# Infini-attention beside a spectral filter: maxima over ScalarE's queue, products with v in two bursts, PSUM banks dealt anew

## The chip, the cores and the metric

One core of a Trainium2 chip runs one program. TensorE (PE, with its weight loads shown as PEld), VectorE (DVE), ScalarE (ACT), GpSimd (POOL) and SyncE (SP, which here only issues DMAs) work side by side, each through its own instructions in order, and wait for each other by semaphores. Matmuls write PSUM, which has 8 banks of 128 x 512 float32; DVE and ACT read it. The metric is the device time of one execution in microseconds, lower is better.

## The reference

Two independent parts whose outputs stand side by side in the last axis. S is 2048, D is 576.

```python
# A: 32 heads of 18, four segments of L = 512
for s in range(4):
    logits = einsum("bhqd,bhkd->bhqk", qs, ks) * scale + causal_mask
    a_dot = einsum("bhqk,bhkd->bhqd", softmax(logits), vs)
    a_mem = einsum("bhld,bhde->bhle", phi(qs), M) / (einsum("bhld,bhd->bhl", phi(qs), z) + 1e-6)
    outs.append(g * a_mem + (1.0 - g) * a_dot)      # g = sigmoid(beta), one per head
    M = M + einsum("bhld,bhle->bhde", phi(ks), vs)
    z = z + phi(ks).sum(over l)
a = concat(outs, heads) @ wo
# B: a filter in frequency
b = irfft2(rfft2(x) * (w_r + 1j * w_i), s=(S, D))
```

## The kernel before

The order of the work is written out by hand: every helper is a generator, and loops step several generators against each other, so the order in the program is the order on each engine. A tile of a pool has a tag with a fixed number of buffers; a new tile of the tag waits until an earlier one has been read by all its readers.

**Stages.** First the forward transform of B (`FFT.forward`, to about 75 us): 16 units u, software-pipelined over 20 steps. `prep` (L118 and on) forms sums and differences eo on DVE, ACT rounds them to eh, and DVE forms the rest el; the third block of eh keeps the rounded value in partitions 0 to 32 and the rest in 64 to 96 (L132, 33 partitions). `f1` multiplies with tables (14 matmuls into two banks), `ev0` (ACT) and `ev1` (DVE) split its result into X0 and X1, `c1` multiplies those (12 matmuls, real and imaginary part in a bank each), and `evz` (ACT, L153) copies them to Z. In step u stand ev0(u-1), evz(u-4), ev1(u-1), f1(u), c1(u-3), with butterfly steps of DVE handed out by a pace counter. PSUM: three pairs for f1 and two single banks for c1.

Then the projections q, k, v of A (to about 283 us), the inverse transform of B together with the start of the attention (to about 357 us), and the attention proper (`attention`, 357 us to the end).

**The attention.** It has 16 units n (segment g = n // 4, eight heads each), halves k = 0 to 31 (four heads each) and steps t = 4k + hh, one head per step. `s1` computes logits with the query on the partitions, ten steps ahead; DVE takes row maxima (L642, L648). `mpath` collects the maxima of four heads (started in the step with hh = 1), PE transposes them (L667, hh = 3), ACT copies them to mts (L670, one buffer), and a DMA (L671) writes them to rows 108 and 109 of the stack Q, so that `s2` subtracts them by matmul, five steps after the transposition at the soonest. `s2` computes logits again with the key on the partitions in three banks (L681; L685 and L686; L690) and ACT takes the exps P0, P1, P2 (L682, L687, L691). After the fourth head POOL zeroes the triangles of P (four selects, L694). `pv` (L709) multiplies by v, four heads side by side in the columns of the array: key block j = 0 two steps after the half's last, j = 1 in the next, j = 3 and 2 in the one after, none in the fourth. `pv_out` copies the sum to U on ACT (L715), `u_dmas` sends it off, `recip` brings back reciprocals of the denominators over DMAs.

A step runs, in this order: two parts of s1 and s2 each (s1 of step t + 10, s2 of step t), pv, `run_bg(1.2)`, the third parts, pv_out, the lanes of reciprocals, `run_bg(0)`. `run_bg` steps the background generators: `den`, `mem1` (memory term), `combine` and `oproj` (output projection) of the segments before. It adds its argument to a counter and does one part when that has reached 1, so every fifth step does a second part, at `run_bg(0)`. PSUM: three banks for s1, three for s2, one for pv and one ("post") for all background parts. s1 has no work left from t = 118 on.

After the steps a drain loop finishes the background, then `last_tile` and `last_proj` finish the last segment, whose reciprocals (rd) come last.

Of the kernel before, what the change touches and what calls it, by code (L numbers as in the profile page):

```python
# [102 lines left out]
class FFT:  # L103
# [4 lines left out]
    def forward(s,xp,cp,pp,wl,xs,consts):  # L108
# [10 lines left out]
        def prep(u,halves=False):  # L119

            x=xin.pop(u)
            eo=xp.tile([128,2,3,128],F32,name="eo",bufs=2)
            h=xp.tile([128,2,3,128],F32R,name="eh",bufs=3)
            for r,op in enumerate((OP.add,OP.subtract)):
                v.tensor_tensor(eo[:,r],x[:,0],x[:,1],op=op)  # L125
                if halves: nc.scalar.copy(h[:,r],eo[:,r])
            if not halves: nc.scalar.copy(h,eo)
            yield
            l=xp.tile([128,2,2,128],F32R,name="el",bufs=3)
            for w in (slice(0,1),slice(1,2)) if halves else (slice(0,2),):  # L130
                v.tensor_tensor(l[:,w],eo[:,w,:2],h[:,w,:2].bitcast(F32),op=OP.subtract)
                v.tensor_tensor(h[64:97,w,2],eo[64:97,w,2],h[64:97,w,2].bitcast(F32),op=OP.subtract)  # L132
            eh[u],el[u]=h,l
            yield
# [16 lines left out]
        def evz(u):  # L151
            a,b=BORD[u]
            for r,p in enumerate(C.pop(u)): nc.scalar.copy(s.Z[:,b,a,r],p[:,:FP])  # L153
        def c1(u):
            a,b=BORD[u]; x=X.pop(u); cc=cw.pop(u)
            for r in range(2):
                p=pp.tile([128,512],F32,name="c1",tag="c1")
                n=0
                for (i,hl) in ((0,0),(0,1),(1,0)):
                    for q in range(2):  # L160
                        k=(0 if q==0 else 2) if r==0 else (1 if q==0 else 0)
                        nc.tensor.matmul(p[:,:FP],cc[:,hl,k*128:(k+1)*128],x[i][:,q],start=n==0,stop=n==5)
                        n+=1
                C.setdefault(u,[]).append(p)
        load(0)
# [219 lines left out]
class ATT:  # L385
# [270 lines left out]
    def mpath(s,k):  # L656

        nc=s.nc; n,qd=divmod(k,2); Q=s.Qs[n%3]
        mx=s.mx.pop(k); mg=s.mg.pop(k)
        nc.vector.tensor_reduce(out=mg[:,:,2:3],in_=mx[:,:,:3],axis=mybir.AxisListType.X,op=OP.max)  # L660
        nc.scalar.copy(mg[:,:,0:1],mx[:,:,3:])
        mh=s.mh; mg=mg.rearrange("p h i -> p (h i)")
        nc.gpsimd.tensor_copy(mh[:,0],mg)
        nc.gpsimd.tensor_tensor(mh[:,1],mg,mh[:,0],op=OP.subtract)
        yield
        pt=s.psm.tile([128,1024],BF,name="mt",tag=s.mtag)[:,:128]
        nc.tensor.transpose(pt,mh.rearrange("p a m -> p (a m)"),s.idb)  # L667
        yield
        mt=s.sm.tile([32,128],BF,name="mts",bufs=1)
        nc.scalar.copy(mt,pt[:32])  # L670
        nc.gpsimd.dma_start(Q[108:110,4*qd:4*qd+4].rearrange("p h (i c) -> p (h i) c",c=128),mt)  # L671
        yield
    def s2(s,t):
# [3 lines left out]
        P=s.P[k]  # L677
# [13 lines left out]
        nc.scalar.activation(P[2][:,hh],p2,AF.Exp,scale=SC)  # L691
        if hh==3:
            def sel(x,pat):
                nc.gpsimd.affine_select(out=x,in_=x,pattern=pat+[[1,128]],compare_op=OP.is_ge,fill=0.0,base=0,channel_multiplier=-1)  # L694
            sel(P[0][:,:,:128],[[0,4]])
            sel(P[1][:,:,:128],[[0,4]])
            sel(P[1][:,:,384:],[[0,4]])
            sel(P[2][:,:,:128],[[0,4]])
        yield
    def pv(s,k,jj):  # L700

        nc=s.nc; n,qd=divmod(k,2); g,G=divmod(n,4)
        P=s.P[k]; vt=s.vs[n]
        if jj==0: s.pvt=s.ps.tile([128,512],F32,name="pv",tag="pv")
        for j in ((0,),(1,),(3,2),())[jj]:
            mv=((P[0],slice(0,512)),(P[1],slice(0,384)),(P[2],slice(0,256)),(P[1],slice(384,512)))[j]
            for hh in range(4):
                h=4*qd+hh
                nc.tensor.matmul(s.pvt[32*hh:32*hh+32,128*j:],vt[:,j,19*h:19*h+32],mv[0][:,hh,mv[1]],start=j==0,stop=j==2,skip_group_check=True)  # L709
# [46 lines left out]
    def den(s,g,lane):  # L756
        nc=s.nc; tp=s.tp
        ds,ds2=[tp.tile([128,512],F32,name=f"ds{i}",tag="ux",bufs=3) for i in range(2)]; ds2=ds2[:32]
        for T,d in ((range(4),ds),((4,),ds2)):
            pd=s.ps.tile([128,512],F32,name="pd",tag="post")  # L760
            for t in T:
                r=126 if t<4 else 72
                nc.tensor.matmul(pd[32*(t%4):32*(t%4)+32],s.zst[g][:r,t],s.pq[g,t][:r],start=True,stop=True,skip_group_check=True)
            nc.scalar.copy(d,pd[:d.shape[0]])
            yield
# [3 lines left out]
        def chain():  # L769
# [3 lines left out]
            yield from s.recip(s.dD[g],s.rdD[g],s.gt,True,"rd",2)  # L773
        lane.append(chain())
    def mem1(s,g,t):
        nc=s.nc; r=126 if t<4 else 72
        pn=s.ps.tile([126,512],F32,name="pn",tag="post")
        nc.tensor.matmul(pn[:r],s.Mst[g][:r,t,:r],s.pq.pop((g,t))[:r],start=True,stop=True)  # L778
# [3 lines left out]
        yield  # L782
        pb=s.ps.tile([126,512],F32,name="pb",tag="post")
        nc.tensor.matmul(pb[:r],s.sel[:,t,:r],s.rc["rd"],start=True,stop=True)
# [15 lines left out]
    def combine(s,g):  # L800
# [14 lines left out]
        for t in range(7+late):  # L815
            if t>1 and not late: high(t-2); low(t-2)
            if t<5:
                r=126 if t<4 else 72; x=xs[t]
                pb=s.ps.tile([126,512],F32,name="pb",tag="post")
                nc.tensor.matmul(pb[:r],s.sel[:,t,:r],s.rc["rr"],start=True,stop=True)  # L820
# [60 lines left out]
    def begin(s,sm,sp,ps1):  # L881
        s.late=[]; s.now=-1
        s.sm,s.sp,s.ps1=sm,sp,ps1
        s.mh=sm.tile([128,8,16],BF,name="mh",bufs=1); s.nc.gpsimd.memset(s.mh,0.0)
        s.mg={};s.mx={};s.m2={};s.P={};s.vs={};s.rc={};s.am={};s.pq={};s.ux={};s.potag="post"
    def prologue(s):
# [20 lines left out]
    def attention(s,tp,ps):  # L907
# [19 lines left out]
        for t in range(133):  # L927
# [24 lines left out]
            steps(a,1)  # L952
            steps(b,1)
            steps(a,1)
            steps(b,1)
# [17 lines left out]
            if qu: qu.pop(0)()  # L973
            run_bg(0)
            s.due(t)
# [142 lines left out]
```

## Time and profile before

| | us |
|---|---|
| median of 3 runs (lowest, highest) | 723.44 (721.72, 724.72) |
| the profiled execution, its own time | 723.62 |
| its span, first to last instruction | 721.9 |
| mean granted clock of TensorE | 0.996 |

Busy shares of the span in 40 slices (tenths; 9 is 90% or more), and the longest pieces by line of the chain that ended last:

```profile
PE   4998999999999999999998999999999999999897
DVE  6999879899699789788587888887566875667433
ACT  3665797585586575444487777777556776567531
POOL 2111000100200112665165334545242762335300
...
PE 75%; DVE 8%; ACT 6%; DMA 5%; issue 3%; POOL 2%; SPq 0%; ACTq 0%; DVEq 0%; POOLq 0%
```

A slice is 18 us. PE is busy nearly everywhere, and the chain is its work for 75% of the span. A busy PE is not PE at its peak: a matmul's record reaches to its modelled end, past the start of the next, so gaps are read from starts in the timeline. A row of the timeline has start and duration in us, engine, line, operation, out<-in, shape, count, and in brackets the idle time before it and what ended that. A row of waits has the waiting instruction, the one waited for, us in total, times, longest.

### The profile page before, as it was taken

To read this page: it belongs to the slowest core of one execution; us is meant where nothing else is said; L and a number is where in the kernel's file an instruction comes from. 1 tells how busy PE (TensorE), PEld (TensorE's weight loads), DVE (VectorE), ACT (ScalarE), POOL (GpSimd) and SP (SyncE) were. 2 spreads that over 40 slices of the span, in tenths; PEclk is the share of its full clock that TensorE was granted. 3 is DMA by queue.
4 is the path that set the end of the run, shared out by engine and by line. 5 is a ranking of instruction groups with operands and counts; after the bars stand their busy time and mean duration, and the time that the engine had idled before them with its cause. 6 is when DMAs were issued, how large, how long until landed. Compare 5 with 4: busy or idle time off the path is not lost.

```text
span 721.9 us, 14482 instructions
## 1 busy us (share of the span) xinstructions
PE 689.0 (95%) x5007; PEld 500.2 (69%) x5007; DVE 551.2 (76%) x1281; ACT 455.2 (63%) x1008; POOL 208.9 (29%) x411
## 2 busy tenths in 40 slices
PE   4998999999999999999998999999999999999897
PEld 4988769879779879999844444444566445664397
DVE  6999879899699789788587888887566875667433
ACT  3665797585586575444487777777556776567531
POOL 2111000100200112665165334545242762335300
PEclk9999999999999999999999999999999999999999
DMA  9884435546363568899547666776546775441142
GB/s 342 268 273 152 132 132 183 176 172 192 102 224 147 176 198 283 204 231 232 166 108 182 172 158 143 177 177 175 128 109 169 177 175 138 111 118 42 34 140 89
DMA packets 83245, 121.06 MB, mean 168 GB/s; under 512 B 11352, under 2 KB 50630, under 8 KB 83036
## 3 DMA queue, kind: packets, MB, share of 16 engines
q1 hardware_dynamic: 76580, 104.11, 50.7%
q0 software_dynamic: 6592, 16.03, 8.1%
q8 instruction: 39, 0.64, 0.4%
q14 instruction: 34, 0.28, 0.1%
HBM read 81.78 MB, written 38.24 MB: 166 GB/s over the span
## 4 chain that ended last, share of the span: by engine, by line
PE 75%; DVE 8%; ACT 6%; DMA 5%; issue 3%; POOL 2%; SPq 0%; ACTq 0%; DVEq 0%; POOLq 0%
PE pj L460 14%; PE pv L709 9%; PE s L638 8%; PE pjv L460 8%; PE po L843 7%; PE i L296 4%; PE i L307 4%; PE s L681 3%; PE s L685 2%; PE pn L778 2%; PE po L872 2%; DVE eo L125 2%; DMA Qs<-mts 2%; PE pm L517 2%; PE s L647 2%
## 5 line engine op out<-in xcount | busy, mean ns | idle before, releaser
L642 DVE CUSTOM_DVE_ANT_0 junk<-s,x 128x512 bf16<-128x512 f32 (+1 forms) x256 | 141.3, 552 | 61.9 <-PE s L638 58.2
L694 POOL TENSOR_SCALAR_AFFINE_SELECT P<-P 128x512 f32<-128x512 f32 x128 | 78.4, 644 | 79.6 <-ACT P L682 72.7
L648 DVE TENSOR_REDUCE mx<-s 128x4 f32<-128x512 f32 x128 | 87.9, 687 | 9.3 <-PE s L647 6.3
L709 PE MATMUL pv<-P,vs 128*32 128x512 f32 (+3 forms) x1024 | 88.8, 442 | 1.0 <-POOL P L694 1.0
L682 ACT ACTIVATE P<-s 128x512 f32<-128x512 f32 x128 | 76.3, 596 | 14.7 <-PE s L681 12.0
L691 ACT ACTIVATE P<-s 128x256 f32<-128x256 f32 x128 | 49.1, 384 | 49.3 <-PE s L690 49.2
L687 ACT ACTIVATE P<-s 128x512 f32<-128x512 f32 x128 | 76.0, 594 | 0.4 <-PE s L686 0.4
L638 PE MATMUL s<-Ks,Qs 108*128 108x384 bf16 (+3 forms) x256 | 69.0, 301 | 1.2 <-DVE mx L648 0.9
L460 PE MATMUL pj<-x,wqkh 128*128 128x512 f32 x162 | 56.5, 409 | 0.0
L638 PEld LDWEIGHTS <-Qs 108*128 108x128 bf16 x320 | 31.5, 99 | 32.8 <-issue 23.4
L206 DVE TENSOR_TENSOR Z<-t,t 128x290 f32<-128x290 f32 (+1 forms) x96 | 48.4, 555 | 0.1
L507 POOL MEMSET vt<- 128x32 f32 x16 | 2.3, 161 | 151.5 <-PE pm L517 124.2
L206 DVE TENSOR_TENSOR t<-Z 128x580 f32<-128x580 f32 x64 | 46.1, 756 | 0.0
L647 PE MATMUL s<-tri,idb 128*128 128x128 bf16 x256 | 43.2, 220 | 0.0
L142 PE MATMUL f<-ftab,eh 128*128 128x290 f32 (+1 forms) x160 | 31.8, 318 | 9.2 <-DMA ftab<-ftab 9.2
L296 PE MATMUL i<-civ,Y 128*128 128x256 f32 (+1 forms) x288 | 39.1, 288 | 0.2 <-POOL Y L281 0.2
L709 PEld LDWEIGHTS pv<-P,vs 128*32 128x32 f32 x1024 | 22.1, 108 | 22.0 <-issue 14.2
L296 PEld LDWEIGHTS i<-civ,Y 128*128 128x128 f32 (+1 forms) x288 | 36.4, 181 | 1.0 <-POOL Y L281 0.4
L638 PE MATMUL s<-Ks,x 108*128 108x384 bf16 (+3 forms) x128 | 35.6, 309 | 0.9 <-DVE mx L648 0.6
L307 PE MATMUL i<-itab,T 128*128 128x290 f32 (+1 forms) x224 | 36.3, 305 | 0.0
L460 PE MATMUL pj<-xh,wqkl 128*128 128x512 f32 x90 | 35.5, 395 | 0.0
L460 PE MATMUL pj<-x,wqkl 128*128 128x512 f32 x90 | 35.5, 395 | 0.0
(202 smaller groups left out, 1813.7 us busy)
## 6 DMA issues: line engine op xcount, KB each, us to landing
qkD<-sp SPq DMA_DIRECT2D x36, 384.0 KB
Ks<-qkD SPq DMA_DIRECT2D x72, 144.0 KB
x<-qkD SPq DMA_DIRECT2D x60, 144.0 KB
Qs<-qkD SPq DMA_DIRECT2D x60, 144.0 KB
xin<-xb SPq DMA_DIRECT2D x16, 384.0 KB
cfw<-cfw POOLq DMA_DIRECT2D x16, 384.0 KB, 4.6
civ<-civ POOLq DMA_DIRECT2D x16, 384.0 KB, 7.4
vs<-vD SPq DMA_DIRECT2D x16, 330.0 KB
```

The source lines that it names most:

```text
L206: v.tensor_tensor(o,a,b,op=op)
L296: nc.tensor.matmul(p[:m,k],Y[i][:,q,c*128:c*128+m],cc[:,hl,o:o+256],start=n==0,stop=n==5)
L307: nc.tensor.matmul(p,x,t,start=n==0,stop=n==6)
L460: s.nc.tensor.matmul(out,a,b,start=i==0,stop=i==len(L)-1)
L638: nc.tensor.matmul(out,Q[:108,h,128*i:128*i+128],K[:108,h,:128*(i+1)],start=True,stop=True)
L642: nc.vector.tensor_tensor_reduce(out=junk[:,:w],in0=src,in1=s.mask[:,512-w:],scale=1.0,scalar=-3.0e38, op0=OP.add,op1=OP.max,accum_out=s.m ...
L647: nc.tensor.matmul(pa[:,o+w-128:o+w],s.idb,s.tri,start=False,stop=True,skip_group_check=True)
L648: nc.vector.tensor_reduce(out=s.mx[k][:,hh],in_=pa.rearrange("p (b c) -> p b c",c=128),axis=mybir.AxisListType.X,op=OP.max)
L682: nc.scalar.activation(P[0][:,hh],p0,AF.Exp,scale=SC)
L687: nc.scalar.activation(P[1][:,hh],p1,AF.Exp,scale=SC)
L694: nc.gpsimd.affine_select(out=x,in_=x,pattern=pat+[[1,128]],compare_op=OP.is_ge,fill=0.0,base=0,channel_multiplier=-1)
L709: nc.tensor.matmul(s.pvt[32*hh:32*hh+32,128*j:],vt[:,j,19*h:19*h+32],mv[0][:,hh,mv[1]],start=j==0,stop=j==2,skip_group_check=True)
```

## The change

Seven edits:

1. `prep`: the subtraction on 33 partitions (L132) goes from DVE to POOL.
2. `c1` writes one tile of two banks, of which there are two; `evz` copies both in one instruction; f1 has two pairs instead of three.
3. `mpath`: in the attention the DMA of the maxima is issued by ACT, at the end of the step after the transposition, instead of by POOL in the step of the transposition. In the prologue it stays.
4. `run_bg(0)` moves from the end of a step to between its first and its second parts of s1 and s2, ahead of `run_bg(1.2)`.
5. `post`: from `now` 117 on, `den`, `mem1`, `combine` and `oproj` take their bank from the three of s1, and so does pv of the last half.
6. In the last steps copies go from ACT to DVE (`pv_out`, the high part of the output projection's input), and the selects of the last half are made for three heads after the third, and for the last head after the fourth.
7. `pv`: key blocks 0 and 3 in the first of its four steps, 1 and 2 in the third, none in the others.

```diff
-                v.tensor_tensor(h[64:97,w,2],eo[64:97,w,2],h[64:97,w,2].bitcast(F32),op=OP.subtract)
+                nc.gpsimd.tensor_tensor(h[64:97,w,2],eo[64:97,w,2],h[64:97,w,2].bitcast(F32),op=OP.subtract)
...
-            for r,p in enumerate(C.pop(u)): nc.scalar.copy(s.Z[:,b,a,r],p[:,:FP])
+            nc.scalar.copy(s.Z[:,b,a],C.pop(u)[:,:,:FP])
         def c1(u):
             a,b=BORD[u]; x=X.pop(u); cc=cw.pop(u)
+            p=C[u]=pp.tile([128,2,512],F32,name="c1",tag="c1")
             for r in range(2):
-                p=pp.tile([128,512],F32,name="c1",tag="c1")
...
-                        nc.tensor.matmul(p[:,:FP],cc[:,hl,k*128:(k+1)*128],x[i][:,q],start=n==0,stop=n==5)
+                        nc.tensor.matmul(p[:,r,:FP],cc[:,hl,k*128:(k+1)*128],x[i][:,q],start=n==0,stop=n==5)
...
-        nc.gpsimd.dma_start(Q[108:110,4*qd:4*qd+4].rearrange("p h (i c) -> p (h i) c",c=128),mt)
+        out=Q[108:110,4*qd:4*qd+4].rearrange("p h (i c) -> p (h i) c",c=128)
+        if s.now<0: nc.gpsimd.dma_start(out,mt)
+        else: s.later(2,lambda: nc.scalar.dma_start(out,mt))
...
-        if hh==3:
-            def sel(x,pat):
-                nc.gpsimd.affine_select(out=x,in_=x,pattern=pat+[[1,128]],compare_op=OP.is_ge,fill=0.0,base=0,channel_multiplier=-1)
...
+        r=slice(0,4) if k<31 else (slice(0,3) if hh==2 else slice(3,4))
+        if hh==3 or k==31 and hh==2:
+            def sel(x):
+                nc.gpsimd.affine_select(out=x[:,r],in_=x[:,r],pattern=[[0,r.stop-r.start],[1,128]],compare_op=OP.is_ge,fill=0.0,base=0,channel_multiplier=-1)
...
-        if jj==0: s.pvt=s.ps.tile([128,512],F32,name="pv",tag="pv")
-        for j in ((0,),(1,),(3,2),())[jj]:
+        if jj==0: s.pvt=s.ps.tile([128,512],F32,name="pv",tag="pv") if k<31 else s.post("pv")
+        for j in ((0,3),(),(1,2),())[jj]:
...
-        s.nc.scalar.copy(s.U[:,qd],s.pvt)
+        (s.nc.vector.tensor_copy if s.now>=117 else s.nc.scalar.copy)(s.U[:,qd],s.pvt)
...
+    def post(s,name):
+
+        p,t=(s.ps1,"s1") if s.now>=117 else (s.ps,"post")
+        return p.tile([128,512],F32,name=name,tag=t)
...
-        pn=s.ps.tile([126,512],F32,name="pn",tag="post")
+        pn=s.post("pn")
...
-            nc.scalar.copy(s.oh[u][:r],s.am[u][:r])
+            (nc.vector.tensor_copy if s.now>=119 else nc.scalar.copy)(s.oh[u][:r],s.am[u][:r])
...
-                ps=s.ps.tile([128,512],F32,name="po",tag=s.potag)[:,:288]
+                ps=(s.ps.tile([128,512],F32,name="po",tag=s.potag) if s.potag else s.post("po"))[:,:288]
...
             steps(a,1)
             steps(b,1)
+            run_bg(0)
             steps(a,1)
             steps(b,1)
             if 4<=t-1<132: s.pv((t-5)//4,(t-5)%4)
...
-            run_bg(0)
             s.due(t)
...
-                pf=es.enter_context(PP(tc,"pf",dict(f1=3,c1=2)))
+                pf=es.enter_context(PP(tc,"pf",dict(f1=2,c1=2)))
```

`s.later(2, f)` calls f at the end of the step after the current one, since `now` still holds the number of the step before.

More of the change, by code (lines that the diff above doesn't have):

```diff
@@ L691, in s2 @@
         nc.scalar.activation(P[2][:,hh],p2,AF.Exp,scale=SC)
-        if hh==3:
-            def sel(x,pat):
[L694 to L698, printed above, removed]
+        r=slice(0,4) if k<31 else (slice(0,3) if hh==2 else slice(3,4))
+        if hh==3 or k==31 and hh==2:
+            def sel(x):
+                nc.gpsimd.affine_select(out=x[:,r],in_=x[:,r],pattern=[[0,r.stop-r.start],[1,128]],compare_op=OP.is_ge,fill=0.0,base=0,channel_multiplier=-1)
+            sel(P[0][:,:,:128])
+            sel(P[1][:,:,:128])
+            sel(P[1][:,:,384:])
+            sel(P[2][:,:,:128])
         yield
@@ L708, in pv @@
                 h=4*qd+hh
-                nc.tensor.matmul(s.pvt[32*hh:32*hh+32,128*j:],vt[:,j,19*h:19*h+32],mv[0][:,hh,mv[1]],start=j==0,stop=j==2,skip_group_check=True)
+                nc.tensor.matmul(s.pvt[32*hh:32*hh+32,128*j:],vt[:,j,19*h:19*h+32],mv[0][:,hh,mv[1]],start=j==0,stop=j>1,skip_group_check=True)
         if jj==3:
@@ L759, in den @@
         for T,d in ((range(4),ds),((4,),ds2)):
-            pd=s.ps.tile([128,512],F32,name="pd",tag="post")
+            pd=s.post("pd")
             for t in T:
@@ L782, in mem1 @@
         yield
-        pb=s.ps.tile([126,512],F32,name="pb",tag="post")
+        pb=s.post("pb")
         nc.tensor.matmul(pb[:r],s.sel[:,t,:r],s.rc["rd"],start=True,stop=True)
@@ L818, in combine @@
                 r=126 if t<4 else 72; x=xs[t]
-                pb=s.ps.tile([126,512],F32,name="pb",tag="post")
+                pb=s.post("pb")
                 nc.tensor.matmul(pb[:r],s.sel[:,t,:r],s.rc["rr"],start=True,stop=True)
@@ L884, in begin @@
         s.mh=sm.tile([128,8,16],BF,name="mh",bufs=1); s.nc.gpsimd.memset(s.mh,0.0)
-        s.mg={};s.mx={};s.m2={};s.P={};s.vs={};s.rc={};s.am={};s.pq={};s.ux={};s.potag="post"
+        s.mg={};s.mx={};s.m2={};s.P={};s.vs={};s.rc={};s.am={};s.pq={};s.ux={};s.potag=None
     def prologue(s):
```

1 line of the change is left out of this document (removed).

## The prediction

> **What bounds the kernel now.** I read the page first, then busy times by stretch, then the timeline of single steps and the lists of waits. Columns of a stretch: its length, busy time of PE, its weight loads, DVE, ACT and POOL with counts, granted clock, DMA share, GB/s.
>
> ```profile
> PE 689.0 (95%) x5007; PEld 500.2 (69%) x5007; DVE 551.2 (76%) x1281; ACT 455.2 (63%) x1008; POOL 208.9 (29%) x411
> 37.71:58.15 20.44, 18.78 (x132) 17.61 (x130) 20.16 (x35) 12.58 (x26) 2.64 (x5) 1.00 0.83 253
> 400.79:408.82 8.03, 8.03 (x76) 3.93 (x74) 6.91 (x22) 6.22 (x16) 3.35 (x8) 1.00 0.64 168
> 391.39:394.81 3.42, 3.42 (x14) 1.63 (x14) 1.95 (x6) 2.60 (x6) 0.61 (x1) 0.50 0.79 217
> ```
>
> PE is the bound almost everywhere. The exceptions are what a change can win: the forward transform from 38 us on, where DVE is busy 20.16 of 20.44 us; a stretch at 391 us where PE ran at clock 0.50; and PE's overhead in a plain group of four steps (8.03 us), in which DVE has 1.1 us and ACT 1.8 us to spare.
>
> **Products with v in two bursts.** The timeline of PE in such a group:
>
> ```profile
> 402.83 0.22 PE L686 MATMUL s<-Qs,Ks 110*128 110x128 bf16 x1
> 402.98 1.06 PE L709 MATMUL pv<-P,vs 128*32 128x512 f32 x8
> 403.97 0.28 PE L638 MATMUL s<-Ks,x 108*128 108x256 bf16 x1
> ...
> 405.30 0.85 PE L709 MATMUL pv<-P,vs 128*32 128x384 f32 x8
> 406.08 0.28 PE L638 MATMUL s<-x,Qs 108*128 108x256 bf16 x1
> ...
> 407.40 0.86 PE L709 MATMUL pv<-P,vs 128*32 128x128 f32 x16
> 408.19 0.28 PE L638 MATMUL s<-x,Qs 108*128 108x256 bf16 x1
> ...
> 651.08 0.06 PE s L686
> ```
>
> From its first start to the next matmul's start a burst takes 0.99 us for 512 columns and 0.78 for 384: 0.21 per 128 columns, so 0.15 is fixed. The third burst, two key blocks of 128 and 256 columns, takes 0.79, as long as one block of 384: joining two blocks costs nothing. Before a burst, L686 holds PE for 0.15 us (402.83 to 402.98); elsewhere the chain of waits gives it the 0.06 of the last row, so 0.09 more belongs to the burst. A burst less saves 0.24 us a group, 7.7 us in 32. Against that stands the step left without a product:
>
> ```profile
> 400.79:402.19 1.40, 1.40 (x14) 0.85 (x12) 1.32 (x4) 1.40 (x5) 1.40 (x4) 1.00 0.60 187
> 404.55:406.65 2.10, 2.10 (x21) 0.93 (x19) 1.80 (x7) 1.55 (x5) 0.41 (x2) 1.00 0.62 153
> ```
>
> The step that has none now lasts 1.40 us; the one that loses its burst has 2.10 - 0.87 = 1.23 without it. If it too grows to 1.40, 0.17 of the 0.24 is lost. In the first, ACT (1.40 of 1.40) also copies the maxima and U; the second has neither, so I take 0.05 lost: 0.19 x 32 = **6.2 us saved** (bounds 2.2 and 7.7).
>
> **Maxima sent by ScalarE.** Starts of L681, the first matmul of a group's exps, and the DMA rows of the chain of waits:
>
> ```profile
> 372.87 0.38 PE L681 MATMUL s<-Qs,Ks 110*128 110x512 bf16 x1
> 391.31 0.56 PE L681 MATMUL s<-Qs,Ks 110*128 110x512 bf16 x1 [1.82 <-DMA Qs<-mts]
> 400.79 0.38 PE L681 MATMUL s<-Qs,Ks 110*128 110x512 bf16 x1
> 374.44 6.90 DMA Qs<-mts
> 384.57 6.70 DMA Qs<-mts
> ```
>
> Groups 2 to 4 last 400.79 - 372.87 = 27.9 us; three plain ones would take 24.1. The 3.8 us are the waits for the maxima, 6.7 to 6.9 us from POOL's issue to PE, and the half clock behind the longer of them (3.42 us at 0.50, 1.7 lost). The issue leaves POOL, where it stands behind four selects, and goes on ACT at the end of the next step:
>
> ```profile
> 402.51 0.37 ACT L691 ACTIVATE P<-s 128x256 f32<-128x256 f32 x1
> 462.77 5.68 DMA rr<-rrD
> L671 POOL DMA_DIRECT2D Qs<-mts x20 | 12.3, 613 | 0.9 <-PE s L681 0.9
> ```
>
> ACT's last exp of that step ends at 402.9; the reader starts at 408.82 (the end of the plain stretch above). That leaves 5.9 us, 5.7 when a group is 0.2 shorter. No DMA of ACT's queue is in this trace. The nearest rows are SP's 96 KB load, 5.68 us to its reader, and POOL's own 6.90; this transfer has 8 KB, so I go by the first, with a little more in the crowded stretch: 6.1 us, 0.25 late in two groups and no half clock. **3.3 us saved** (bounds: 3.8 if it lands in time, 0 at 6.9 us). The issue itself costs ACT at most POOL's 0.61 us; queued behind it are the exps of the next step, and its cover is ACT's 1.8 idle us a group and the burst of 1.3 us that comes in that step. Without the cover 30 x 0.61 = 18 us would show; I take 0. The next copy into the one mts buffer, four steps later, waits for the landing as well, with the same slack.
>
> **Forward transform: bank pairs, and 33 rows of eh on POOL.** c1 has two pairs instead of two single banks and so waits for ACT's copy of the unit before the last; f1 has two pairs instead of three and must wait for DVE's subtraction two units back.
>
> ```profile
> 45.78 1.90 PE L162 MATMUL c<-X,cfw 128*128 128x290 f32 x12 [0.36 <-ACT Z L153]
> 49.91 1.88 PE L162 MATMUL c<-X,cfw 128*128 128x290 f32 x12 [0.33 <-ACT Z L153]
> 69.31 3.48 PE L162 MATMUL c<-X,cfw 128*128 128x290 f32 x24 [0.77 <-ACT Z L153]
> 73.52 1.88 PE L162 MATMUL c<-X,cfw 128*128 128x290 f32 x12 [0.73 <-ACT Z L153]
> L132 DVE TENSOR_TENSOR eh<-eo,eh x18: 289/422/423, 6.8 to 62.4; 33x256 fp32r<-33x256 f32 x14, 33x128 fp32r<-33x128 f32 x4
> ```
>
> A step lasts 4.13 us (45.78 to 49.91) because DVE does; the waits for Z at 45 and 49 would become waits of f1 for DVE, with c1 and the next f1 queued behind. Those at 69.31 and 73.52 have no DVE behind them: 0.77 + 0.73 = 1.5 us go. Whether DVE gets shorter by L132's 0.42 us in its last six steps (2.5 us) hangs on POOL:
>
> ```profile
> L739 POOL TENSOR_TENSOR ry<-ry,rw 128x128 f32<-128x128 f32 x8 | 3.7, 464 | 23.6 <-ACT rw L738 23.5
> L813 POOL TENSOR_TENSOR ol<-am,oh x10: 1263/1272/1277, 473.1 to 594.8; 126x512 fp32r<-126x512 f32 x8, 72x512 fp32r<-72x512 f32 x2
> L813 DVE TENSOR_TENSOR ol<-am,oh x5: 681/686/1161, 659.9 to 678.0; 126x512 fp32r<-126x512 f32 x4, 72x512 fp32r<-72x512 f32 x1
> 659.53 3.12 POOL L694 TENSOR_SCALAR_AFFINE_SELECT P<-P 128x512 f32<-128x512 f32 x4 [0.53 <-ACT P L682]
> 668.78 2.48 POOL L694 TENSOR_SCALAR_AFFINE_SELECT P<-P 128x512 f32<-128x512 f32 x4 [5.56 <-ACT P L682]
> ```
>
> Between 464 ns for 128 elements and 1272 for 512, 256 take POOL some 0.73 us. And the two engines get in each other's way: DVE's L813, 0.69 us in the median, took up to 1.16, the first time at 659.9, where POOL's four selects took 3.12 us instead of the 2.48 of the next four. So DVE may lose 0.47 and win 0.42. I take nothing from this edit, **1.5 us saved** in all (bounds: 4.0 if POOL's work is free; 0.4 lost if DVE stands still for the whole 0.73, six times 0.31 against 1.5).
> The Trainium skill (SBUF — State Buffer, "SBUF: two separate sides") speaks against the edit: a DVE operation with two inputs in SBUF and a POOL operation that reads SBUF exclude each other for the whole instruction. By it the sum would take the last bound, 1.9 us above mine. The trace agrees that they exclude each other, and shows 0.47 us of it.
>
> **Background parts and banks.** Waits of PE in 469 to 655 us, then in 655 to 722 us:
>
> ```profile
> PE pb L820 <- DVE am L785: 1.1, 2, 0.6
> PE pb L820 <- DVE ux L825: 0.6, 1, 0.6
> PE pd L763 <- DVE am L785: 0.6, 1, 0.6
> ```
>
> ```profile
> PE pv L709 <- POOL P L694: 1.0, 1, 1.0
> PE po L843 <- DVE am L785: 0.8, 1, 0.8
> PE pb L820 <- DVE am L785: 0.6, 1, 0.6
> PE po L843 <- ACT ob L845: 0.5, 1, 0.5
> PE pb L784 <- ACT am L780: 0.5, 1, 0.5
> ```
>
> The first list is the fifth-step part that asks for the one bank of "post" right behind the other part: 2.3 us. Half a step later most is over, but in a step without products the next part follows closer; half, **1.2 us saved** (bounds 0 and 2.3). In the second list the bank waits, 2.4 us, go with three banks, and of POOL's 1.0 about 0.7, as the three earlier heads are selected a step earlier: **3.1 us saved** (bounds 1.5, if another wait follows, and 3.7, with ACT's copies gone to DVE). DVE takes some ten copies of 0.69 us there; PE has work queued behind all of them.
>
> **The sum.** 6.2 + 3.3 + 1.5 + 1.2 + 3.1 = 15.3 us. The profiled execution took 723.62 us (span 721.9 and 1.7 around it), the median of the runs is 723.44. 723.6 - 15.3 = **708.3 us**.
>
> **Rivals.**
> (a) The maxima land late in every plain group. ACT issues 0.9 us after POOL did. At 6.9 us each landing is 1.2 us after the 5.7 us; some 13 groups are as short as the plain one, 15.6 us. With the early gain gone: 708.3 + 3.3 + 15.6 = 727 us, slower. It passes the old time from 5.7 + 12/13 = 6.6 us on. For it are the 6.9 and 6.7; against it that they fell in a crowded stretch (DMA share 0.79 against 0.64 in the plain group), and the 5.68 of a transfer twelve times as large.
> The Trainium skill (DMA: Bandwidth & Descriptors, "Issuing engines are not separate DMA queues") says that DMAs of all engines run on the same 16 engines and another issuer saves only its time to issue; by it the 6.9 us would stay, which is this rival.
> (b) Two bursts starve ACT and DVE and feed them too fast after: each new step without products takes 1.40 us. 4 us of the gain go: 712 us. For it is the 1.40; against it the free time of DVE and ACT in the group.
> (c) DVE stands still for POOL in the forward transform: 710.2 us. For it is the 1.16; against it that DVE's other work there reads PSUM.
> (d) Forward relief comes whole, with the upper bounds of the banks: 708.3 - 2.5 - 1.1 - 0.6 - 1.5 (bursts) = 702.6 us.
>
> **How the numbers follow.** Forecast 0.45, (a) 0.13, (b) 0.17, (c) 0.12, (d) 0.13. A measurement tells about 0.5% from no change: 719.8 to 727.1 us counts as the same. (a) spreads around its 727 us and gives slower 0.08 and the same 0.05; 0.03 for the same comes from mixtures of (a) and (b). Range 700 to 721 us, the forecast's own 704 to 713.
>
> **What would show it.** Two bursts of L709 a group, 1.25 and 1.2 us long, and a plain group of 7.8 to 7.9 us. No L681 waiting for mts before 395 us, no clock of 0.50 there. c1 with no wait for Z at the end of the forward transform; L131 or L206 of DVE stretched by 0.3 or more would be (c). No wait of po and pb for DVE or ACT after 655 us. L681 waiting for mts in most groups would prove me wrong in sign.

## The result and the profile after

| | before | after |
|---|---|---|
| median of 20 runs each, us (lowest, highest) | 723.10 (721.31, 724.72) | 719.90 (714.79, 727.59) |
| ratio after / before, 95% interval | | 0.9956 (0.9943 to 0.9970) |
| the profiled execution, us (span) | 723.62 (721.9) | 718.92 (717.2) |

The change gains 3.2 us where 15.3 were forecast: 0.44%, with an interval that does not reach 1. The runs after spread more than those before; the one of 727.59 us counts as slow and is not in the ratio.

The page of the changed kernel, first the row of busy times, then its row of a DMA queue that was not there before:

```profile
PE 684.1 (95%) x5007; PEld 505.7 (71%) x5007; DVE 552.3 (77%) x1270; ACT 450.1 (63%) x985; POOL 211.1 (29%) x403
...
q10 hardware_dynamic: 1020, 0.25, 0.2%
```

PE's busy time fell by 4.9 us, as the span by 4.7. The new queue is ACT's: 30 transfers of 34 packets.

Where it came from is read by stage. First matmul of the projections (the forward transform's end), before and after:

```profile
75.24 0.40 PE L460 MATMUL pj<-x,wqkh 128*128 128x512 f32 x1
```

```profile
73.61 0.40 PE L459 MATMUL pj<-x,wqkh 128*128 128x512 f32 x1
```

Then the attention in stretches cut at the first exps of a half (columns as in the prediction: length, busy time of PE, its loads, DVE, ACT, POOL, then clock, DMA share and GB/s). Before: a plain group and its four steps, halves 2 to 5, 12 to 19, and 31 with the drain up to the last projection.

```profile
416.86:424.90 8.04, 8.04 (x76) 3.94 (x74) 6.91 (x22) 6.22 (x16) 3.36 (x8) 1.00 0.72 163
...
418.26:420.62 2.36, 2.36 (x19) 0.93 (x18) 1.99 (x8) 1.80 (x5) 0.47 (x1) 1.00 0.59 131
420.62:422.73 2.11, 2.11 (x21) 0.94 (x19) 1.81 (x7) 1.56 (x5) 0.41 (x2) 1.00 0.71 188
422.73:424.90 2.17, 2.17 (x30) 1.21 (x28) 1.79 (x6) 1.47 (x4) 1.09 (x2) 1.00 0.93 182
372.87:408.82 35.95, 33.82 (x295) 16.30 (x293) 28.33 (x88) 27.11 (x65) 17.90 (x32) 0.95 0.71 173
460.21:553.03 92.82, 89.47 (x731) 49.87 (x728) 62.79 (x182) 59.98 (x144) 36.48 (x69) 1.00 0.60 149
669.07:700.99 31.92, 29.22 (x214) 20.65 (x212) 13.28 (x19) 13.46 (x32) 7.96 (x14) 1.00 0.27 76
```

The same of the changed kernel, and behind them a stretch at half clock:

```profile
414.73:422.70 7.97, 7.97 (x76) 4.11 (x74) 6.91 (x22) 6.11 (x16) 2.85 (x7) 1.00 0.64 179
414.73:416.13 1.40, 1.40 (x14) 0.86 (x11) 1.32 (x4) 1.40 (x5) 0.88 (x2) 1.00 0.62 163
416.13:418.71 2.58, 2.58 (x28) 1.19 (x27) 1.99 (x8) 1.80 (x5) 0.00 (x0) 1.00 0.62 159
418.71:420.06 1.35, 1.35 (x14) 0.82 (x12) 1.34 (x5) 1.26 (x4) 0.41 (x2) 1.00 0.62 171
420.06:422.70 2.64, 2.64 (x30) 1.25 (x28) 2.25 (x8) 1.64 (x5) 1.56 (x3) 1.00 0.70 212
371.15:406.96 35.81, 32.45 (x295) 16.42 (x293) 28.22 (x90) 26.73 (x66) 16.65 (x31) 1.00 0.69 167
457.85:551.80 93.95, 89.16 (x730) 51.64 (x728) 62.67 (x182) 60.22 (x144) 31.55 (x60) 0.98 0.61 150
666.94:696.13 29.19, 28.32 (x213) 21.20 (x212) 14.97 (x23) 11.08 (x26) 7.77 (x17) 1.00 0.30 83
508.11:511.52 3.41, 3.41 (x19) 1.55 (x22) 1.82 (x5) 2.12 (x4) 0.85 (x2) 0.50 0.45 123
```

The forward transform gave 1.63 us and the end 2.73 (31.92 to 29.19). A plain group is 0.07 us shorter. Halves 2 to 5, where the maxima should have won 3.3 us, are as long as before, halves 12 to 19 are 1.1 us longer, and halves 20 to 27 are 1.3 us shorter (90.64 to 89.35). PE's waits for transfers of 0.8 us and more in 455 to 552 us, which holds halves 12 to 19:

```profile
PE pd L765 <- DMA pq<-pqD: 1.4, 1, 1.4
PE pb L826 <- DMA rr<-rrD: 1.2, 1, 1.2
PE s L682 <- DMA Qs<-mts: 0.8, 1, 0.8
```

Three transfers came late, and behind the first, a wait of 1.4 us ended at 507.1, lies the half clock: 3.41 us, 1.7 lost.

### The profile page after: what moved, and what is told of

The parts are those of the page before. It is cut to its first block, busy times and chain, and to the rows that moved or that the text cites. A ratio compares the mean times of both kernels' runs of the same rounds, so it can differ in the third digit from the quotient of the medians.

```text
span 717.2 us, 14460 instructions
## 1 busy us (share of the span) xinstructions
PE 684.1 (95%) x5007; PEld 505.7 (71%) x5007; DVE 552.3 (77%) x1270; ACT 450.1 (63%) x985; POOL 211.1 (29%) x403
## 5 line engine op out<-in xcount | busy, mean ns | idle before, releaser
L696 POOL TENSOR_SCALAR_AFFINE_SELECT P<-P 128x512 f32<-128x512 f32 (+2 forms) x132 | 78.8, 623 | 67.3 <-ACT P L683 51.8
L711 PE MATMUL pv<-P,vs 128*32 128x512 f32 (+3 forms) x1024 | 82.8, 441 | 0.0
L711 PEld LDWEIGHTS pv<-P,vs 128*32 128x32 f32 x1024 | 27.2, 109 | 45.3 <-issue 42.5
L142 PEld LDWEIGHTS f<-ftab,eh 128*128 128x128 f32 (+1 forms) x160 | 26.2, 207 | 14.1 <-issue 8.5
```

Of the source, the lines that this page charges most:

```text
L142: nc.tensor.matmul(p[:,r,:FP],x,t,start=n==0,stop=n==6)
L696: nc.gpsimd.affine_select(out=x[:,r],in_=x[:,r],pattern=[[0,r.stop-r.start],[1,128]],compare_op=OP.is_ge,fill=0.0,base=0,channel_multiplie ...
```

## The experiments

Ratios are to the kernel before, run on the same chip beside them, five rounds each. "POOL kernel" is the changed kernel with the maxima's DMA back on POOL, at the old place. A profile shows one run; in the runs with the bursts alone, with the issue one step earlier, with SyncE, with the issue ahead of the selects and in both with the late loads of pq it is the kernel's longest.

### Each part alone in the kernel before

Products with v in two bursts (edit 7) alone:

```diff
-        for j in ((0,),(1,),(3,2),())[jj]:
+        for j in ((0,3),(),(1,2),())[jj]:
...
```

(The rest is the flag that ends the sum.)

> The kernel before with the products with v in two bursts and nothing else. Forecast's step: 6.2 us less, a plain group of 7.85 us. Rival (b), as the changed kernel's plain group of 7.97 us suggests (the step left without a product takes 1.35 instead of 1.23): 0.07 us in each of some 16 plain groups and 0.24 in the others, in which background work fills the gaps, 1.1 + 3.8 = 4.9 us less at most, 2 us if the others gain no more than the plain ones.

The maxima over ACT (edit 3) alone:

```diff
-        nc.gpsimd.dma_start(out,mt)
+        if s.now<0: nc.gpsimd.dma_start(out,mt)
+        else: s.later(2,lambda: nc.scalar.dma_start(out,mt))
```

> The kernel before with the maxima sent by ACT at the end of the next step and nothing else. Forecast's step: 3.3 us less, no L681 waiting for mts after the first one. Late landing: in the changed kernel the first data packet follows ACT's issue by 1.3 to 5.8 us, and groups 2 to 5 there take 35.8 us against 36.0 before; so 0 us, between 1 us less and 3 us more, with waits for mts of 2 to 4 us in all and a wider spread of the runs.

The move of `run_bg(0)` (edit 4) alone:

```diff
             steps(b,1)
+            run_bg(0)
             steps(a,1)
...
-            run_bg(0)
             s.due(t)
```

> The kernel before with the second background part in the middle of the next step and nothing else. Forecast's step: 1.2 us less. Rival: the two parts of den now follow each other within one step, the second asks for the fifth pq tile before its load (6 us from issue) has landed, PE waits 1.4 us for it and, if the idle is long enough, runs at clock 0.50 for 3.4 us: 0 to 3 us more.

The forward transform's edits (1 and 2) alone:

```diff
-                v.tensor_tensor(h[64:97,w,2],eo[64:97,w,2],h[64:97,w,2].bitcast(F32),op=OP.subtract)
+                nc.gpsimd.tensor_tensor(h[64:97,w,2],eo[64:97,w,2],h[64:97,w,2].bitcast(F32),op=OP.subtract)
...
-                pf=es.enter_context(PP(tc,"pf",dict(f1=3,c1=2)))
+                pf=es.enter_context(PP(tc,"pf",dict(f1=2,c1=2)))
```

> The kernel before with the subtraction of 33 rows on POOL and the bank pairs in the forward transform and nothing else. Forecast's step: 1.5 us less, the changed kernel's own first product of the projections comes 1.63 us sooner, so 1.6 us less if nothing behind it waits for something else. DVE's step of 4.1 us stays as long as before if POOL's work holds DVE up as much as it takes off it.

The last steps' edits (5 and 6) alone: banks, copies and selects of the end.

```diff
...
-            pd=s.ps.tile([128,512],F32,name="pd",tag="post")
+            pd=s.post("pd")
...
```

> The kernel before with the banks of s1 for the background and the last half from step 117 on, the copies on DVE and the split selects, and nothing else. Forecast's step: 3.1 us less, and the same in the stretch from the last exps to the end; the changed kernel gains 2.7 us from its group 30 on. Less than 1.5 us would mean that the reciprocals' way through DMAs sets the end instead of PE.

| part | forecast, us (bounds) | measured ratio (95%) | gain, us |
|---|---|---|---|
| two bursts | 6.2 (2.2 to 7.7) | 0.9979 (0.9958 to 1.0000) | 1.5 |
| maxima by ACT | 3.3 (0 to 3.8) | 1.0030 (1.0010 to 1.0050) | -2.2 |
| forward transform | 1.5 (-0.4 to 4.0) | 0.9992 (0.9976 to 1.0008) | 0.6 |
| background parts | 1.2 (0 to 2.3) | 0.9968 (0.9952 to 0.9983) | 2.3 |
| last steps | 3.1 (1.5 to 3.7) | 0.9951 (0.9932 to 0.9970) | 3.5 |

The gain is (1 - ratio) x 723. The five sum to 5.7 us. Two terms failed, the bursts in size and the maxima in sign; the other three come to 6.4 us where 5.8 were forecast. The stretches agree: with the last steps' edits alone, half 31 with the drain takes 28.84 us instead of 31.92; with the move alone, halves 12 to 27 take 180.9 us instead of 183.5.

### Parts taken out of the change

The maxima back on POOL, at the old place:

```diff
-        if s.now<0: nc.gpsimd.dma_start(out,mt)
-        else: s.later(2,lambda: nc.scalar.dma_start(out,mt))
+        nc.gpsimd.dma_start(out,mt)
```

> The changed kernel with the maxima sent by POOL in the step of the transposition as before. If ACT's late issue is what costs (late landing), this is 1 to 3 us faster than the changed kernel (some 717 to 719 us), with a narrower spread. If the issuer doesn't matter, 720 us. If the forecast's 3.3 us are there and something else ate them, 723 us.

715.52 us, ratio 0.9912 (0.9881 to 0.9943): by the ratios 3.2 us less than the changed kernel, by the medians, each taken beside its own runs of the kernel before, 4.4. One edit takes back about half of what the others win.

ACT's issue one step earlier, `s.later(1,...)` for `s.later(2,...)`:

> The changed kernel with ACT's issue one step earlier, at the end of the step of the transposition, 2 us more time to land. Late landing: L682 no longer waits for mts but for one or two cases, 2 to 4 us faster than the changed kernel, 716 to 718 us, and the spread narrows to before's 3 us. If ACT's time for the issue (0.62 us) is what costs, there is no gain, or a loss, since it now stands behind the U copy in the step in which ACT is fullest.

725.03 us, 1.0023 (1.0002 to 1.0043): slower, with no wait for the maxima left at all. ACT's timeline shows why; ACTq is the issue, in the bracket the time ACT did nothing, and what ended it:

```profile
388.59 0.57 ACT L717 COPY U<-pv 128x512 f32<-128x512 f32 x1
390.91 0.62 ACTq L672 DMA_DIRECT2D Qs<-mts  x1
391.63 0.60 ACT L683 ACTIVATE P<-s 128x512 f32<-128x512 f32 x1 [2.47 <-DMA uD<-U]
```

The maxima are ready at 388.7, and yet the issue stands until 390.9, when a transfer of U has landed, with all exps behind it. "The issue itself costs ACT at most POOL's 0.61 us" was wrong: it costs that, and what an earlier transfer is late. In this profile five of the 30 issues stood for 0.8 to 1.9 us.

`run_bg(0)` back at the end of the step:

> The changed kernel with the second background part back at the end of its step. If the move costs (den's second part asks too soon for its tile), 1 to 3 us faster than the changed kernel and no wait of pd for pq; if the move is worth the forecast's 1.2 us, 1.2 us slower.

720.72 us, 0.9965 (0.9937 to 0.9993): 0.6 us over the changed kernel's ratio, inside both intervals; this doesn't tell the move's worth in place; alone it was worth 2.3 us.

### What of ACT's issue costs

Two kernels part the place from the engine: SyncE issues at ACT's place, and POOL at ACT's place.

```diff
-        else: s.later(2,lambda: nc.scalar.dma_start(out,mt))
+        else: s.later(2,lambda: nc.sync.dma_start(out,mt))
```

> The changed kernel with the maxima's DMA issued by SyncE at the same place of the program (end of the step after the transposition), nothing else changed. The changed kernel took 719.9 us, with POOL as the issuer at the old place 715.5 us. Theory 1 (the loss is ACT itself: its issue stands in order among the exps, takes 0.62 us there and waits for transfers issued before it): 715 to 717 us, no exp late behind an issue, plain groups 7.97 us. Theory 2 (the loss is the later issue, 0.9 us behind POOL's, so that the maxima land late): 719 to 721 us, with the same 3 us of waits of s2's first matmul for mts in groups 2 to 5. Theory 3 (the hardware-issued transfers themselves take longer beside the loads): as theory 2, and worse where SyncE's loads stand behind it.

720.9 us, 0.9979 (0.9962 to 0.9996).

```diff
-        else: s.later(2,lambda: nc.scalar.dma_start(out,mt))
+        else: s.later(2,lambda: nc.gpsimd.dma_start(out,mt))
```

> The changed kernel with the maxima's DMA issued by POOL, but at the place where ACT issues it now, one step after the transposition. It parts the place from the engine. Theory 1 (ACT's own time): within 1 us of POOL at the old place, 715 to 717 us. Theory 2 (the place): s2's first matmul waits for mts in most groups, some 0.9 us longer than with POOL at the old place; 718 to 726 us. By theory 3 (hardware-issued transfers) as theory 1.

714.94 us, 0.9894 (0.9869 to 0.9919): the best of all versions, beside one below that equals it, and by the ratios 4.5 us less than the changed kernel, from which it differs by one word. So the place isn't the price: POOL pays nothing there, and theory 2 falls. SyncE's run doesn't settle theory 1, that it is ACT's own time: SyncE has the loads to issue, and what it loses may be its own. The same stretch of waits, 455 to 552 us, with POOL:

```profile
PE s L682 <- DMA x<-mts: 0.4, 1, 0.4
PE s L637 <- DMA Ks<-qkD: 0.4, 1, 0.4
PE pb L826 <- DMA rr<-rrD: 0.4, 1, 0.4
```

```profile
458.80:548.19 89.39, 87.48 (x728) 51.16 (x728) 62.07 (x180) 59.45 (x143) 35.66 (x67) 1.00 0.61 155
```

The second fence is the stretch of halves 12 to 19: 89.4 us, against 93.95 in the changed kernel; the waits for pq, rr and maxima (3.4 against 0.8) and the 1.7 us of half clock make 4.3 of the 4.6. Most of that is loads that SyncE issues. For the maxima PE waits as long with POOL as with ACT in 355 to 420 us, first the changed kernel, then POOL at ACT's place:

```profile
PE s L682 <- DMA Qs<-mts: 2.4, 2, 1.4
```

```profile
PE s L682 <- DMA Qs<-mts: 2.3, 2, 1.4
```

With SyncE the waits are elsewhere, on Q and rr; a list of PE and one row of SyncE's:

```profile
PE pb L826 <- DMA rr<-rrD: 3.0, 1, 3.0
PE s L637 <- DMA Qs<-qkD: 2.4, 1, 2.4
```

```profile
SPq L672 <- ACT mts L669: 5.0, 1, 5.0
```

SyncE stood 5 us for one copy of the maxima, until 363.4 us. PE's two waits ended at 402.9 and 471.4 us; what made those loads late isn't shown.

That an issue on ACT can be held is seen in the changed kernel's chain of waits from 392 to 408 us (start, us, what):

```profile
392.89 8.27 DMA Qs<-qkD
...
401.24 5.59 DMA x<-mts
```

ACT's last exp ended at 399.8; the issue waited until 401.2, when a load of Q, into another tile, had landed, and the next exps waited behind it. Loads, issue and maxima stand in a row. But this is the only one of the 30 issues that starts more than 0.12 us behind ACT's work before it, and PE then waited for these maxima for 0.25 us. An instruction that waits for a semaphore stands ahead of 25 of the 30 issues on ACT, and of 21 of the 30 on POOL at the same place. In these traces the semaphores that tell of the landing of ACT's transfers tell of SyncE's loads too; those of POOL's transfers tell of POOL's alone. One of PE's longer waits for the maxima came behind an issue that nothing held, while ACT's last exp still ran:

```profile
372.67 0.65 ACTq L672 DMA_DIRECT2D Qs<-mts  x1
```

```profile
380.26 0.39 PE L682 MATMUL s<-Qs,Ks 110*128 110x512 bf16 x1 [0.97 <-DMA Qs<-mts]
```

From issue to reader that is 7.6 us, and in the two other waits of over 0.5 us 7.8 and 8.5. With POOL at the same place the three are 7.7, 7.5 and 7.9. So these profiles don't show the maxima landing later over ACT than over POOL.

The last kernel of this kind keeps the maxima with POOL at ACT's place and lets ACT issue a useless transfer of the same tile beside it:

```diff
-        else: s.later(2,lambda: nc.scalar.dma_start(out,mt))
+        else: s.later(2,lambda: (nc.gpsimd.dma_start(out,mt),nc.scalar.dma_start(s.xD[k%2],mt)))
```

> The changed kernel with the maxima issued by POOL at ACT's place (714.9 us), and beside it ACT issues a transfer of the same mts tile to a scratch tensor in device memory that nobody reads (30 times 8 KB); the output does not depend on it. Theory H (one more hardware-queue transfer a group holds the issue of others): 718.5 to 721 us, with waits of SyncE for the landing of these transfers and of ACT at its issue, and PE waiting for pq, rr, Q or K. Theory M (the maxima land late): 714.5 to 716 us.

715.76 us, 0.9909 (0.9881 to 0.9937): within theory M's range, no difference from POOL alone that can be told, and by the ratios 3.4 us less than the changed kernel. ACT issues at the same place here, though for 0.31 us instead of 0.62, and is held as well; this issue starts 1.3 us behind the exp before it:

```profile
401.41 0.37 ACT L693 ACTIVATE P<-s 128x256 f32<-128x256 f32 x1
403.08 0.31 ACTq L673 DMA_DIRECT2D xD<-mts  x1
```

SyncE waits for landings in both; the longest row of its waits for the maxima, in the changed kernel, and for the useless transfers here:

```profile
SPq L621 <- DMA Qs<-mts: 4.2, 4, 1.9
```

```profile
SPq L622 <- DMA xD<-mts: 4.0, 3, 2.5
```

In all it waits 8.3 us there and 5.3 here, and here no time is lost. So theory H falls, and theory 1 with it: neither one more transfer on ACT's queue nor ACT's being held at its issue is the price by itself. Theory M is what is left of the theories, but the waits above don't bear it out. How ACT's issue of the maxima costs its 3 to 4.5 us stays open. Part of it is half clock: the mean granted clock of the runs is 0.9972 in the changed kernel and 0.9993 with POOL at ACT's place, which is some 1.5 us, an estimate from these two. And it doesn't come every time: the changed kernel's fastest run took 714.79 us. One thing that differs in the useless transfer is its row on the page:

```profile
q10 hardware_dynamic: 1440, 0.25, 0.2%
```

It has 48 packets each and not 34. The Trainium skill (DMA: Bandwidth & Descriptors, "Why a DMA increments its semaphore by 16 and not by 1") says that a transfer runs on the largest number of engines up to 16 that divides the outer dimension on both sides, and that a hardware queue takes the lowest-numbered ones: two for the maxima (two rows of Q), sixteen for the useless transfer. The counts agree, if each engine adds one packet (32 + 2, 32 + 16). Whether the two lowest engines are crowded, and the loads or the maxima late by that, was not tried.

### Is the early stretch bound by its transfers?

POOL's issue of the maxima, put ahead of the four selects instead of behind them:

```diff
         nc.scalar.activation(P[2][:,hh],p2,AF.Exp,scale=SC)
+        yield
...
             if hh==3 and m is not None: steps(m,1)
+            steps(b,1)
```

> The changed kernel with POOL as the issuer of the maxima, and the issue put ahead of the four selects of the half on POOL, instead of behind them: 1.4 to 2 us earlier. If the early groups' 2.0 us of waits for mts are a matter of the issue's time, they go: 713.5 us (712.5 to 715), no waits of s2's first matmul for mts. If the transfer takes as long as the other transfers leave it, whatever its issue, the waits stay and the time is 715.5 us. If the selects are now late for the first burst of products: a wait of that burst for POOL in most groups and over 717 us.

721.14 us, 0.9982 (0.9961 to 1.0004): slower than the POOL kernel, though no wait for the maxima is left. PE's waits from 355 to 420 us, and the stretch behind the first:

```profile
PE s L637 <- DMA Ks<-qkD: 2.6, 1, 2.6
```

```profile
404.70:408.12 3.42, 3.42 (x21) 1.64 (x22) 2.75 (x8) 2.50 (x5) 0.00 (x0) 0.50 0.62 142
```

Halves 2 to 4 are 1.6 us shorter than in the POOL kernel, and half 5 is 4.1 us longer: PE reaches keys that are not there yet, and 3.4 us of half clock follow. Halves 28 to 30 are 4.1 us longer too (29.9 to 25.8): there a burst of half 30 waited 1.6 us for POOL's selects, which now stand behind the issue, with half clock behind it again.

Then five loads of pq are taken out of that stretch, in the changed kernel and with POOL at ACT's place:

```diff
-            if 16<=t<21: s.pq_load(1,t-16)
+            if 24<=t<29: s.pq_load(1,t-24)
```

> The changed kernel, with the five loads of pq for the second segment (252 KB each in the first four) issued in steps 24 to 28 instead of 16 to 20; den needs them from step 34 on. Theory A (groups 2 to 5 are bound by what the transfers bring, so that maxima, Q and K wait for each other there): fewer waits for mts and for Q and K before 410 us, groups 2 to 5 at most 34 us instead of 35.8, 717 to 718.5 us. Theory B (the waits come from the maxima's issue on ACT alone): groups 2 to 5 stay at 35 to 36 us and the time at 719.5 to 720.5 us.

719.77 us, 0.9960 (0.9934 to 0.9987).

> The same move of the five loads, in the changed kernel with the maxima issued by POOL at ACT's place (714.9 us). Theory A: groups 2 to 5 fall from 35.0 to 33 or less, 713 us (712 to 714). Theory B: 714.5 to 715.5 us. If the loads now collide with what comes after step 24: 716 us and more, with waits for Q or K behind 410 us.

716.17 us, 0.9903 (0.9880 to 0.9925). No gain in either, where theory A had 717 to 718.5 us and 713. In the profiles halves 2 to 5 take 33.2 us (35.8 with the loads at their old place) and 33.5 (35.0), and halves 6 to 19 give it back, 154.4 (144.8) and 143.9 (141.1). But both profiles are of the kernel's longest run, and the versions with POOL as the issuer and the loads at their old place took 33.6 to 35.0 us for halves 2 to 5. So the fall isn't certain even for the stretch, and that the same bytes are waited for later isn't shown.

### What the bursts are worth in place

The POOL kernel with three bursts:

> The changed kernel with POOL as the issuer of the maxima at the old place and the products with v in three bursts as before: it shows what the two bursts are worth where nothing else disturbs. From the plain groups (8.04 us with three bursts, 7.97 with two) 0.07 us x 32 = 2.2 us, so 717.8 us. By the prediction (0.19 us a group) 6.2 us, so 721.7 us. If the bursts are worth nothing: 715.5 us.

715.87 us, 0.9917 (0.9897 to 0.9936), against 0.9912 with two: no difference that can be told. By stages two bursts win 1.2 us in halves 12 to 19 (91.2 to 90.0), beside background parts, 0.1 in halves 6 to 11 (51.2 to 51.1), and lose 0.5 in halves 28 to 30 (25.3 to 25.8).

Products behind the third part of s1, so that DVE has a tile to work on in a burst:

```diff
-            if 4<=t-1<132: s.pv((t-5)//4,(t-5)%4)
             run_bg(1.2)
             steps(a,1)
+            if 4<=t-1<132: s.pv((t-5)//4,(t-5)%4)
```

> The changed kernel with the maxima issued by POOL at ACT's place, and the products with v placed behind the third part of s1 of the same step instead of ahead of it. If DVE, which has nothing to do during most of a burst of 1.2 us and then holds s1's banks, is what takes back the gain of the two bursts: steps without product go from 1.40 and 1.35 to about 1.28, plain groups from 7.97 to 7.8 us, 712 to 713 us. If the step without product is bound by ACT's exps instead: no change, 714.5 to 715.5 us.

716.76 us, 0.9917 (0.9890 to 0.9945). A plain group and its new step without products:

```profile
415.98:424.12 8.14, 8.14 (x77) 4.11 (x75) 6.91 (x21) 6.11 (x16) 3.45 (x8) 1.00 0.69 171
419.99:421.35 1.36, 1.36 (x14) 0.83 (x12) 1.10 (x2) 1.27 (x4) 0.41 (x2) 1.00 0.63 149
```

The step keeps its length though DVE is busy for only 1.10 us of it (1.34 of 1.35 in the changed kernel), so it is not DVE's work that fills it; ACT has 1.27 of 1.36, which was not tried. The steps with bursts grew.

Two bursts in halves 11 to 27 only, three in the others:

```diff
-        for j in ((0,3),(),(1,2),())[jj]:
+        for j in (((0,3),(),(1,2),()) if 11<=k<28 else ((0,),(1,),(3,2),()))[jj]:
```

> The changed kernel with the maxima issued by POOL at ACT's place, two bursts of products only in halves 11 to 27 and three bursts, as before the change, in the others. If two bursts pay only beside background parts: 713.5 to 714.5 us, halves 28 to 30 at 25.3 us instead of 25.8. If they pay everywhere: 716 us.

714.87 us, 0.9897 (0.9875 to 0.9919). Halves 28 to 30 take 25.21 us, as expected. But halves 12 to 19, with two bursts, took 91.0 us in this profile, as much as with three above: sums of stages vary by more than the bursts are worth, and where these pay isn't settled.

### The 33 rows on POOL

With POOL at ACT's place, the subtraction is back on DVE:

> The changed kernel with the maxima issued by POOL at ACT's place, and the subtraction on 33 rows back on DVE. If the relief of DVE is worth what DVE's instructions take (0.42 us in each of the last steps): the projections start 1 to 2.5 us later, 716 to 717 us. If POOL and DVE only hold each other up (rival c): they start earlier by up to 1.9 us. If neither, within 0.3 us at the start of the projections, 714.9 us.

715.92 us, 0.9906 (0.9884 to 0.9927), which can't be told from 714.94. PE's waits up to the projections have this row in the changed kernel and, to the digit, with the subtraction on DVE:

```profile
PE f L142 <- DVE X L149: 2.5, 5, 1.2
```

The projections start at 74.22 us, against 74.66 with the subtraction on POOL, and PE's wait for the tables at the very start differs by as much (10.0 and 10.5 us). Edit 1 does neither good nor harm that can be measured. Why it does no good is in part in the timeline: where DVE's next subtraction meets POOL's, it takes longer. The changed kernel, then the one with the subtraction on DVE:

```profile
36.21 0.92 POOL L132 TENSOR_TENSOR eh<-eo,eh 33x256 fp32r<-33x256 f32 x1 [2.06 <-ACT eh L127]
36.45 1.23 DVE L131 TENSOR_TENSOR el<-eo,eh 128x512 fp32r<-128x512 f32 x1
```

```profile
37.07 0.68 DVE L131 TENSOR_TENSOR el<-eo,eh 128x512 fp32r<-128x512 f32 x1
```

DVE is rid of 0.42 us and L131 takes 0.55 us longer, in five of its 18 instances. From one such L131 to the next a step takes 4.10 us in both kernels.

## Why the prediction was wrong

**The sum.** The working was right in kind for three terms of five, and 9.5 of the 15.3 us stood in the two that failed.

**Two bursts.** Held: bursts of 1.25 and 1.2 us (measured 1.21, 416.92 to 418.13, and 1.22, 420.85 to 422.07). A burst less saves 2.56 - 2.43 = 0.13 us (three bursts of 0.99, 0.78 and 0.79 against two), near the 0.15 called fixed. Not held: "the second has neither, so I take 0.05 lost". The new step without a product lasts 1.35 us and not 1.28 or less, and the step behind it takes 2.64 - 1.22 - 0.09 = 1.33 without its burst where before it was 2.17 - 0.79 - 0.09 = 1.29. With 0.12 in the one step, 0.04 in the other and 0.02 in the bursts, some 0.17 of the 0.24 is lost. 0.07 us is saved, the lower bound that I had written down, 2.2 us in 32 groups; alone the edit gave 1.5 us, and in place nothing that can be told. That is rival (b), at the price it named (4 us). Of its reason, DVE and ACT starved by the burst and fed too fast after, DVE's part fell in the run with the products placed later; ACT's was not tried.

**Maxima by ACT.** Two steps failed. The first is the base, what there was to win: "the 3.8 us are the waits for the maxima" came from one execution. With the maxima untouched, halves 2 to 5 took 34.7 us with the move alone, 34.6 with the bursts, 34.9 with the last steps' edits and 33.9 with the forward edits, against 35.95 in the profile I read; the half clock at 391 us is in none of them. Against four plain groups, 32.2 us, that is 1.7 to 2.7 us of waits. The second is the landing, "6.1 us, 0.25 late in two groups and no half clock": where PE waited, it took 7.6 to 8.5 us from issue to reader, as long as over POOL, so there was no gain. And "I take 0" for ACT's issue was no price at all for what stands ahead of it. The term came out as a loss, 2.2 us alone and 3.2 in place (4.5 against POOL at ACT's place). That the issuer is the price is shown; by what way is not. Rival (a), the later issue, fell with POOL at ACT's place; the maxima are late here and there, not in every plain group.

**Forward transform.** Held: 1.5 us forecast, 1.63 at the first projection in the profiles, and PE's waits for Z are gone; waits of f1 for DVE stand in their place, as said. DVE and POOL: nothing, as taken, and for the reason given: "DVE may lose 0.47 and win 0.42" was 0.55 and 0.42. The sign named for rival (c), L131 stretched by 0.3 or more, came; its loss of 1.9 us did not. The estimate of 0.73 us for POOL's work was short, it took 0.92 to 1.24. The Trainium skill (SBUF — State Buffer, "SBUF: two separate sides") says that the two exclude each other for a whole instruction; the stretched L131 agrees, and no loss of time followed in the run with the subtraction back on DVE. Alone, the gain is not certain in the runs (0.9992, with 1 in its interval).

**Background parts and last steps.** Held, both near their upper ends: 2.3 of 2.3, and 3.5 of 3.7. Of PE's waits behind 655 us in the changed kernel this one answers to those of before:

```profile
PE po L849 <- DVE am L786: 0.7, 1, 0.7
```

The bank waits of pb are gone; one of po for DVE stays, which the list of what would show it had excluded.

**What would show it.** The two bursts came as long as said, the plain group of 7.8 to 7.9 us did not (7.97). "No L681 waiting for mts before 395 us" failed (0.97 us at 380.3, and 1.4 us at 397.9), "no clock of 0.50 there" held, but a stretch of it came at 508. "L681 waiting for mts in most groups" did not come, and the sign of the term was wrong all the same.

## What to carry to other kernels

A wait read from one execution is a sample: where it is a transfer's, look at the same stretch in other kernels' profiles before its whole length is booked as a gain. Price an issue by what may stand ahead of it in the chain of waits, not by its 0.6 us alone: one step earlier, the same issue stood for 0.8 to 1.9 us five times, with ACT's exps behind it. Where one word chooses the engine that issues a transfer, try the others: POOL was 4.5 us better than ACT at the same place, and no row of the profile before tells of it. Time won on one transfer can be waited for on the next: with the waits for the maxima gone, PE stood 2.6 us for keys.

## What the hardware showed

An issue on ACT took 0.62 us (0.61 on POOL), and was harmless where nothing held it (plain groups last 7.97 us with ACT and with POOL as the issuer); where an earlier transfer held it, ACT stood idle for 1.5 to 2.5 us in the kernel that issues a step earlier. Half clock followed waits of PE for transfers of 1.4 us (changed kernel, 3.41 us long) and 2.6 us (issue ahead of the selects, 3.42), but not this one of 1.7 us, with POOL at ACT's place, at 580 us:

```profile
PE s L682 <- DMA Qs<-mts: 1.7, 1, 1.7
```

The Trainium skill (TensorE: Matmul & The Clock Gate, "Part 1: The HAM clock gate") gives about 3.4 us of idle time for it; the stretches here are as long as that, but the waits ahead of them were shorter.

A DVE subtraction that met one of POOL's took 1.23 us instead of 0.68, and POOL's took 0.92 to 1.24 us.
